# Moving the decoding of the last weights between experts, and three weight splits into the conv layer

## The chip, the core and the metric

The kernel runs on one core of one Trainium2 chip. The metric is the device time of one execution in microseconds (us): 430.35 as the median of 3 runs of the kernel before (429.88 to 430.53). Engines: PE is TensorE, ACT is ScalarE, DVE is VectorE, POOL is GpSimd, SP is SyncE, which here issues DMAs.

## What is computed

Three layers stand one behind the other, on 2 sequences of 768 tokens with 512 values each: a linear attention with decay, a mixture of 8 experts of which each token takes one, and a gated conv layer. Cut to what matters here:

```python
def _moe_ref(x, w_gate, w_local, w1, w2):
    ...
            e = ...                          # one expert for each token
            h = np.maximum(x[b, s] @ w1[e], 0.0)
            out[b, s] = p[e] * (h @ w2[e])

def _moe2_ref(x, w_in, conv_w, w_out):
    h = np.maximum(x @ w_in, 0.0)            # 512 -> 1024
    ...                                      # conv_out: 3 taps along the tokens
    gate = 1.0 / (1.0 + np.exp(-conv_out))
    return (h * gate @ w_out)                # 1024 -> 512
```

w1 is 8 x 512 x 1024, w2 is 8 x 1024 x 512, w_in is 512 x 1024 and w_out is 1024 x 512.

## The kernel before

**Products in three parts.** Every product of the two later layers is made from two parts of each operand: a high part `hi` (ACT copies the f32 value into the reduced f32r type) and the rest `lo` (DVE subtracts `hi` from the value). PE adds hi x hi, hi x lo and lo x hi. For weights this is a split: `split_first` (line 174) makes `whi` on ACT, `split_second` (line 183) makes `wlo` on DVE and then asks for the next load, and `split_unit` does both. A unit is a tile of 128 x 1024 values. There are 64 units of expert weights, 8 for each expert (4 of w1, 4 of w2), loaded by SP into a ring of 4 raw tiles, and then 8 units of the conv layer (4 of w_in, 4 of w_out). `whi` and `wlo` lie in rings of 10 tiles each, so a split waits until PE is done with the unit ten places before it.

**Decoding.** w_in and w_out arrive as 64-bit floats and have to be decoded into f32 first. `decode` (lines 198 to 228) works on half a unit, 128 x 512, 16 times in all. Its first part, `dec_first`, is two ACT instructions (lines 216, 217). Its second part, `dec_second`, is five DVE instructions (lines 219 to 225), two POOL instructions, a product and a sum (lines 227, 228), and a load of 512 KB on SP (line 245) into one of two `draw` tiles. Called with the pool `mo`, the two scratch tiles are one tile `dmf` with two buffers, which it shares with `hr`; called without, they are `dmag` and `df` with one buffer each. The scratch tile `ds` has one buffer. The results are the tiles `wdec`, in the pool `dp`, which is closed before the conv layer.

**The experts.** Experts 1 to 6 run in the first layer `L1(e)` and the second layer `L2(e)`, on 256 tokens. `L1` has four steps `dt` of 24 matmuls; after each but the last a unit is split, and in the last step ACT and DVE make `hh` and `hl`, the two parts of the hidden values, from the banks. Then `T(e + 1)` turns the next expert's tokens (`xsh`, `xsl`), one or two units are split, and `L2` has four steps `j` of 12 matmuls with a split after each. Experts 0 and 7 run in `alone`, in two halves of 128 tokens: four steps for each half `f` of the hidden values (line 652), then ACT's `hr` (line 663), turned back by PE (line 640) into `hh` and `hl`, then eight steps `ft` (line 671), and at the end the result `ys`, half copied by DVE, half by ACT, and stored. `alone` yields after each step, and the calling loop puts other work between. In expert 0 a branch for overflowing tokens (`overflow`) is passed over in this data; its body names the same buffers as `ys`, `hr` and `dmf`.

**Where the decodings stand before.** Expert 0: two, at steps 5 and 6 of its first half. `L1(e)`: one begun at step 2 for e > 1, ended in `L2(e)` at step 1. `L2(e)`: one begun at step 3, ended at step 0 of the next `L1`. Expert 7: three, begun at steps 1, 5 and 10 of its first half. That is 2 + 5 + 6 + 3 = 16.

**Into the conv layer.** After the first half of expert 7, POOL gathers the first sequence's rows (`c_gather`, line 954); during the second half `c_scale` scales them (tiles 0 to 3 on DVE, 4 and 5 on ACT), and `c_T` turns them (line 936) into a bank of the ring "a", which has two banks; ring "b" has three. ACT and DVE read the bank out into the window tiles `x` (lines 946, 949). The last six splits, of which four are of w_out, stand in this half too. The conv layer, `moe2`, runs `h2` (line 979: 12 matmuls for one hidden tile, then `hs`, `cs`, `sg`, `gh` and `gl` on ACT and DVE) and `o2` (line 1031), in the order h2(0, all), h2(1, first four), o2(0), h2(1, last four), o2(1) and so on.

Each engine runs its instructions in the order in which the program writes them, and so do the DMA queues; the order is written out by hand.

Of the kernel before, what the change touches and what calls it, by code (L numbers as in the profile page):

```python
# [8 lines left out]
F32 = mybir.dt.float32  # L9
# [13 lines left out]
E = 8  # L23
P = 128
# [18 lines left out]

WBUFS = 10
DEC_STEP = 10
SPLIT_STEPS = (4, 5, 6, 7, 8, 9)
# [53 lines left out]
def tile_kernel(ctx: ExitStack, tc: tile.TileContext, consts, qk, kv, w1, w2, w_in, conv_w, w_out, out):  # L100
# [87 lines left out]
    def split_unit(engine=None):  # L188
        if nxt["split"] < len(units):
            split_first()  # L190
            split_second(engine or nc.vector)
# [3 lines left out]
    dp = dst.enter_context(tc.tile_pool(name="dp", bufs=1))  # L195
    wdec = [dp.tile([P, 1024], F32, name=f"wdec{j}") for j in range(KD + KF // 2)]

# [64 lines left out]
    def dec_second(queue=nc.sync):  # L262
        if "g" in dec_raw:
            for _ in dec_raw.pop("g"):
                pass
            dec_load(queue)
# [336 lines left out]
    def moe(mo):  # L603
# [25 lines left out]
        def alone(e, half, free):  # L629
# [37 lines left out]
            for ft in range(KF):  # L667
                wh, wl = split[e * 8 + KD + ft // 2]
                ws = slice((ft % 2) * DM, (ft % 2 + 1) * DM)
                for a, b_ in ((hh, wh), (hh, wl), (hl, wh)):  # L670
                    nc.tensor.matmul(yp, lhsT=a[:, ft, sl], rhs=b_[:, ws], start=(ft == 0 and a is hh and b_ is wh),  # L671
                                     stop=(ft == KF - 1 and a is hl))
                if ft == 0:
                    back(1)
                if ft % 2 and free:
                    split.pop(e * 8 + KD + ft // 2)
                    split_unit()
                if ft < KF - 1:
                    yield
# [10 lines left out]
        def L1(e):  # L690
# [3 lines left out]
            for dt in range(KD):  # L694
                wh, wl = split[e * 8 + dt]
                if dt == 0:
                    dec_second()
                elif dt == 1:
                    next(rest, None)
                elif dt == 2 and e > 1:  # L700
                    dec_first(mo)
# [18 lines left out]
        def L2(e):  # L720
# [3 lines left out]
            for j in range(KF // 2):  # L724
                wh, wl = split[e * 8 + KD + j]
                if j == 1:
                    dec_second()
                elif j == 2:
                    next(rest, None)
                elif j == 3:  # L730
                    dec_first(mo)
                for jj in range(2):
# [41 lines left out]
        for n, _ in enumerate(first):  # L774
            if n in (0, 1, 2, 5):
                split_unit(nc.vector)
            if n == 4:
                T(0, (1,))
            if n == 3:
                overflow(mo)  # L780
            if n == 5:
                dec_first()
            elif n == 6:
                dec_first(mo)
            elif n == 7:
                dec_second()
# [15 lines left out]
        e = E - 1  # L802
        for n, _ in enumerate(alone(e, 0, False)):
            if n in (1, 5, 10):
                dec_first()
            if n in (3, 8, 13):
                dec_second()
        raw0 = [dp.tile([P, 2, DM], F32, name="yg0", tag="draw", bufs=2) for _ in range(2)]
# [4 lines left out]
        for n, _ in enumerate(alone(e, 1, True)):  # L813
            if n >= 8 and n - 8 < NC:
                c_scale(n - 8)
            if n == 7:
                window(1, [wp.tile([P, 1024], F32R, name="x2", tag=tag) for tag in ("whi", "whi", "wlo", "wlo")])
            if 10 <= n < 14:
                c_T(0, n - 10)

# [110 lines left out]

    def c_T(b, c):
        y = yg_t.pop(b * NC + c)
        p_ = bank("a")
        for dt in range(KD):
# [22 lines left out]
    def moe2(fo):  # L958
# [98 lines left out]
        for ft in range(KF):  # L1057
# [3 lines left out]
            if 1 <= ft <= NC:  # L1061
                c_gather(NC - 1 + ft, fo.tile([P, DM], F32, name="yg", tag="yg", bufs=6))
        h2(1, 0, KF // 2)
        drain()
# [154 lines left out]
```

## Time and profile before

| what | value |
|---|---|
| median of 3 runs | 430.35 us (429.88 to 430.53) |
| the profiled execution, device time | 430.57 us |
| its span, first to last instruction | 428.8 us |
| PE busy | 394.6 us, 92% of the span |
| DVE busy | 285.7 us, 67% |
| ACT busy | 250.9 us, 59% |
| POOL busy | 114.3 us, 27% |
| PE's share of the chain that ended last | 64% |

Busy shares are means over the whole span. The stages have different limits, so the table by stretches, the chain and the timeline of single engines have to be read beside them. In a timeline the bracket behind an instruction is the time for which its engine sat idle before it, and what ended that. The granted clock of PE is 1.00 at 2.4 GHz and 0.50 at 1.2 GHz.

### The profile page before, as it was taken

The page shows a single profiled execution, that of the slowest core. Times are in us where ns is not written, and L with a number is a line of the kernel's source. Part 1 is how long each engine was busy: PE and PEld are TensorE (multiplying, and loading weights), DVE is VectorE, ACT ScalarE, POOL GpSimd, SP SyncE. Part 2 cuts the span into 40 slices and gives each one's busy share as a digit, 9 for nine tenths or more (in the row PEclk, how much of TensorE's full clock was granted, in tenths as well). Part 3 has the DMA queues.
Part 4 walks back from the last instruction along what each step waited for, and adds up shares of the span by engine and source line. Part 5 has one row for each costly group of instructions (what it writes and reads, how often), then busy time and mean ns, then how long its engine had stood idle before and what let it go on. Part 6 is the DMA issues. An engine that isn't in the chain of part 4 may idle for free.

```text
span 428.8 us, 7360 instructions
## 1 busy us (share of the span) xinstructions
PE 394.6 (92%) x2772; PEld 340.3 (79%) x2772; DVE 285.7 (67%) x540; ACT 250.9 (59%) x489; POOL 114.3 (27%) x109
## 2 busy tenths in 40 slices
PE   5989898949999999999999949779999999999996
PEld 2778776637989898988989828559988989998986
DVE  1457877766797999887778764676990734992250
ACT  3777654627475766566756531657875635982441
POOL 3343450334005044554644442715000000000000
PEclk9999999997999999999999987999999999999999
DMA  7999995376869797888886140324101001001001
GB/s 265 305 318 354 383 326 209 110 240 240 300 213 300 216 311 277 303 281 273 289 266 224 53 141 0 99 74 125 48 0 75 1 26 50 2 0 49 26 0 73
DMA packets 28231, 73.37 MB, mean 171 GB/s; under 512 B 3025, under 2 KB 3793, under 8 KB 28194
## 3 DMA queue, kind: packets, MB, share of 16 engines
q1 hardware_dynamic: 19506, 54.67, 37.2%
q10 hardware_dynamic: 6384, 10.68, 6.8%
q0 software_dynamic: 2304, 7.54, 5.9%
q8 instruction: 22, 0.36, 0.3%
q14 instruction: 15, 0.12, 0.1%
HBM read 62.39 MB, written 10.49 MB: 170 GB/s over the span
## 4 chain that ended last, share of the span: by engine, by line
PE 64%; DVE 5%; ACT 3%; issue 2%; DMA 2%; POOL 2%; ACTq 0%; POOLq 0%; DVEq 0%
PE c L739 15%; PE c L1031 14%; PE b L979 9%; PE b L707 8%; PE rt L979 4%; PE state L707 4%; PE rt L707 4%; PE a L583 1%; PE b L1031 1%; PE c L671 1%; DMA raw<-in_moe_w_dram 1%; DMA yg<-scr,posi 1%; PE a L936 1%; DVE ds L222 1%; DVE wlo L183 1%
## 5 line engine op out<-in xcount | busy, mean ns | idle before, releaser
L183 DVE TENSOR_TENSOR wlo<-raw,whi 128x1024 fp32r<-128x1024 f32 x64 | 81.2, 1282 | 23.4 <-ACT whi L174 22.0
L174 ACT CAST whi<-raw 128x1024 fp32r<-128x1024 f32 x64 | 66.8, 1054 | 39.3 <-PE c L739 22.1
L998 DVE SCALAR_TENSOR_TENSOR cs<-hs,cw,cs 128x384 f32<-128x384 f32 x64 | 39.6, 620 | 32.9 <-ACT cs L996 31.8
L227 POOL TENSOR_TENSOR dmf<-dmf,ds 128x512 f32<-128x512 f32 x12 | 23.2, 1934 | 90.6 <-DVE ds L225 60.1
L739 PE MATMUL c<-whi,hh 128*112 128x512 f32 x96 | 38.0, 396 | 0.0
L979 PE MATMUL b<-x,whi 128*128 128x386 f32 x168 | 35.8, 341 | 1.9 <-ACT x L946 1.6
L739 PE MATMUL c<-wlo,hh 128*112 128x512 f32 x96 | 37.5, 390 | 0.0
L1031 PE MATMUL c<-whi,gh 128*128 128x512 f32 x88 | 35.0, 398 | 0.0
L1031 PE MATMUL c<-whi,gl 128*128 128x512 f32 x88 | 34.8, 395 | 0.0
L1031 PE MATMUL c<-wlo,gh 128*128 128x512 f32 x88 | 34.7, 394 | 0.0
L979 PEld LDWEIGHTS b<-x,whi 128*128 128x128 f32 x168 | 29.5, 189 | 3.3 <-ACT x L946 2.1
L739 PE MATMUL c<-whi,hl 128*112 128x512 f32 x96 | 29.6, 390 | 0.0
L707 PE MATMUL b<-xsh,whi 128*128 128x240 f32 x96 | 26.5, 276 | 0.0
L707 PE MATMUL b<-xsl,whi 128*128 128x240 f32 x96 | 26.5, 276 | 0.0
L707 PE MATMUL b<-xsh,wlo 128*128 128x240 f32 x96 | 26.3, 274 | 0.0
L611 POOL DMA_INDIRECT xg<-scr,permi x15 | 18.4, 1227 | 25.8 <-DVE nbi L542 18.8
L357 DVE TENSOR_TENSOR A<-b,C 128x512 f32<-128x512 f32 x24 | 15.5, 686 | 14.3 <-PE b L351 14.3
L228 POOL TENSOR_TENSOR wdec<-dmf 128x512 f32<-128x512 f32 x12 | 22.5, 1871 | 0.9
L1002 ACT ACTIVATE sg<-cs 128x384 f32<-128x384 f32 x32 | 16.7, 522 | 8.4 <-DVE gl L1008 8.0
L739 PEld LDWEIGHTS c<-whi,hl 128*112 128x112 f32 x96 | 17.4, 181 | 4.5
L739 PEld LDWEIGHTS c<-whi,hh 128*112 128x112 f32 x96 | 17.4, 181 | 4.3
L739 PEld LDWEIGHTS c<-wlo,hh 128*112 128x112 f32 x96 | 17.4, 181 | 4.2
(228 smaller groups left out, 1025.9 us busy)
## 6 DMA issues: line engine op xcount, KB each, us to landing
raw<-in_moe_w_dram SPq DMA_DIRECT2D x64, 512.0 KB, 5.4
qk<-in_qk_dram SPq DMA_DIRECT2D x11, 512.0 KB
kv<-in_kv_dram SPq DMA_DIRECT2D x11, 512.0 KB, 6.8
draw<-in_moe_w_in_dram SPq DMA_DIRECT2D x8, 512.0 KB, 5.7
draw<-in_moe_w_out_dram SPq DMA_DIRECT2D x8, 512.0 KB, 5.4
scr<-xo ACTq DMA_DIRECT2D x11, 256.0 KB, 5.7
out_dram<-os ACTq DMA_DIRECT2D x11, 256.0 KB, 2.6
scr<-ys ACTq DMA_DIRECT2D x10, 256.0 KB
```

The lines of the kernel that those rows point to most:

```text
L174: nc.scalar.copy(hi, raw[u])
L183: engine.tensor_tensor(out=lo, in0=t, in1=hi.bitcast(F32), op=ALU.subtract)
L227: nc.gpsimd.tensor_tensor(out=f, in0=f, in1=s.bitcast(F32), op=ALU.mult)
L228: nc.gpsimd.tensor_tensor(out=out, in0=f, in1=a.bitcast(F32), op=ALU.add)
L357: nc.vector.tensor_tensor(out=A_t[i][j], in0=sc2[j].rearrange("p (a t) -> p a t", a=NP), in1=cv("mask").unsqueeze(1).to_broadcast([P, NP, ...
L611: nc.gpsimd.indirect_dma_start(out=t, out_offset=None, in_=xrow, in_offset=bass.IndirectOffsetOnAxis(ap=permi[:, col:col + 1], axis=0))
L707: nc.tensor.matmul(o, lhsT=a[:, fs], rhs=b_[:, dt, OFF:], start=(dt == 0 and n == 0 and ft % 2 == 0), stop=(dt == KD - 1 and n == 2), skip ...
L739: nc.tensor.matmul(yp[t][0:P - o], lhsT=a[:, ft, t * P + o:(t + 1) * P], rhs=b_[:, ws], start=(ft == 0 and a is hh and b_ is wh), stop=(ft ...
L979: nc.tensor.matmul(pb[:, 0:WN], lhsT=split[u_in + dt][wi][:, fs], rhs=x_[dt // 2][:, dt % 2, :], start=(n == 0), stop=(n == 3 * KD - 1))
L998: nc.vector.scalar_tensor_tensor(out=cs, in0=tap[j], scalar=cw[:, j, ft:ft + 1], in1=cs, op0=ALU.mult, op1=ALU.add)
L1002: nc.scalar.activation(out=sg, in_=cs, func=AF.Sigmoid)
L1031: nc.tensor.matmul(ops[t][:, 0:n_], lhsT=a[:, ts_], rhs=b_[:, ws], start=(ft == 0 and n == 0), stop=(ft == KF - 1 and n == 2))
```

## The change

The 16 decodings are dealt out anew: one in expert 0; two in each of experts 1 and 2 (begun in `L1` at step 2 and in `L2` at step 3); three in each of experts 3, 4 and 5 (`L1` at steps 0 and 2, `L2` at step 2); two in expert 6 (`L1` at steps 0 and 2); none in expert 7. From expert 3 on each is ended one step after it begins, apart from that of `L1`'s step 2, which is ended at step 1 of `L2`. The last three units (`KEPT`) are no longer split in expert 7 but in the conv layer: one after h2(0) has done tile 5, two within the first part of h2(1). Their `wdec` tiles lie in the pool `cst`, which stays open. `c_T` in expert 7 uses the rings "a" and "b" in turn, and the scalings on ACT (tiles 4 and 5) come after the turning of tiles 2 and 3, not before.

```diff
+DENSE = 3
+KEPT = 3
...
-    wdec = [dp.tile([P, 1024], F32, name=f"wdec{j}") for j in range(KD + KF // 2)]
+    n_dec = KD + KF // 2
+    wdec = [(dp if j < n_dec - KEPT else cst).tile([P, 1024], F32, name=f"wdec{j}") for j in range(n_dec)]
...
                 if ft % 2 and free:
                     split.pop(e * 8 + KD + ft // 2)
-                    split_unit()
+                    if nxt["split"] < len(units) - KEPT:
+                        split_unit()
...
                 if dt == 0:
                     dec_second()
+                    if e >= DENSE:
+                        dec_first(mo)
                 elif dt == 1:
                     next(rest, None)
-                elif dt == 2 and e > 1:
+                    dec_second()
+                elif dt == 2:
                     dec_first(mo)
...
                 elif j == 2:
                     next(rest, None)
+                    if DENSE <= e < E - 2:
+                        dec_first(mo)
                 elif j == 3:
-                    dec_first(mo)
+                    if e < DENSE:
+                        dec_first(mo)
+                    else:
+                        dec_second()
...
             if n == 5:
                 dec_first()
-            elif n == 6:
-                dec_first(mo)
             elif n == 7:
                 dec_second()
...
-        for n, _ in enumerate(alone(e, 0, False)):
-            if n in (1, 5, 10):
-                dec_first()
-            if n in (3, 8, 13):
-                dec_second()
+        for _ in alone(e, 0, False):
+            pass
...
         for n, _ in enumerate(alone(e, 1, True)):
-            if n >= 8 and n - 8 < NC:
+            if 8 <= n < 12:
                 c_scale(n - 8)
...
             if 10 <= n < 14:
-                c_T(0, n - 10)
+                c_T(0, n - 10, "ab"[n % 2])
+            if n in (12, 13):
+                c_scale(n - 8)
...
-    def c_T(b, c):
+    def c_T(b, c, ring="a"):
         y = yg_t.pop(b * NC + c)
-        p_ = bank("a")
+        p_ = bank(ring)
...
+            if ft == 5:
+                split_unit()
-        h2(1, 0, KF // 2)
+        for ft in range(KF // 2):
+            h2(1, ft, ft + 1)
+            if ft in (0, 2):
+                split_unit()
         drain()
```

## Rows read from the trace of the kernel before

**Rows 1.** Stretches: length, busy PE, PEld, DVE, ACT, POOL (instructions), PE clock, DMA share, GB/s.

```profile
90.70:97.20 6.50, 0.00 (x0) 0.00 (x0) 4.07 (x6) 2.20 (x5) 4.29 (x4) 0.79 0.51 177
97.20:101.10 3.90, 3.85 (x11) 3.23 (x12) 2.94 (x3) 2.54 (x4) 2.77 (x3) 0.50 0.46 161
...
176.00:198.60 22.60, 22.60 (x154) 20.35 (x154) 18.30 (x25) 14.71 (x20) 11.73 (x7) 1.00 0.86 286
243.80:285.90 42.10, 29.91 (x129) 21.90 (x127) 24.84 (x44) 18.73 (x35) 18.84 (x15) 0.92 0.27 81
257.50:261.50 4.00, 3.96 (x12) 3.29 (x13) 2.12 (x5) 0.59 (x1) 0.00 (x0) 0.50 0.00 0
285.90:313.00 27.10, 26.88 (x152) 25.85 (x153) 21.72 (x51) 20.81 (x45) 6.00 (x6) 1.00 0.23 68
313.00:428.80 115.80, 112.22 (x577) 99.88 (x576) 56.52 (x113) 61.20 (x129) 0.00 (x0) 1.00 0.07 28
```

**Rows 2.** The chain that ended last: start, length in us, what.

```profile
105.27 2.76 PE c L671 x12
...
165.04 10.95 PE c L739 x48
...
187.69 10.95 PE c L739 x48
```

**Rows 3.** Timelines around the first expert's wait: start, length, engine, instruction [idle before].

```profile
90.76 0.67 ACT L216 ACTIVATE dmf<-draw 128x512 f32<-128x512 f32 x1 [4.35 <-DMA raw<-in_moe_w_dram]
...
90.81 1.28 POOL L227 TENSOR_TENSOR df<-df,ds 128x512 f32<-128x512 f32 x1 [6.54 <-remote]
...
95.21 0.42 DVE L681 COPY ys<-c 128x256 f32<-128x256 f32 x1
...
97.25 1.11 PE L640 MATMUL a<-C,hr 128*128 128x128 f32 x4 [6.59 <-ACT hr L663]
```

**Rows 4.** Timelines of the last expert: PE, ACT and POOL.

```profile
253.66 0.49 PE L671 MATMUL c<-whi,hl 128*128 128x512 f32 x1 [2.47 <-DVE hl L644]
257.54 1.11 PE L640 MATMUL a<-C,hr 128*128 128x128 f32 x4 [3.38 <-ACT hr L663]
...
255.79 0.66 ACT L216 ACTIVATE dmag<-draw 128x512 f32<-128x512 f32 x1 [5.82 <-POOL wdec L228]
...
271.90 1.19 POOL L954 DMA_INDIRECT yg<-scr,posi  x1 [0.79 <-DMA scr<-ys]
```

**Rows 5.** Timelines of POOL and DVE where their instructions meet.

```profile
180.88 2.14 POOL L227 TENSOR_TENSOR dmf<-dmf,ds 128x512 f32<-128x512 f32 x1 [3.55 <-DVE ds L225]
...
182.53 1.58 DVE L183 TENSOR_TENSOR wlo<-raw,whi 128x1024 fp32r<-128x1024 f32 x1 [0.66 <-ACT whi L174]
...
252.92 0.68 DVE L644 TENSOR_TENSOR hl<-a,hh 128x512 fp32r<-128x512 f32 x1
...
253.15 1.27 POOL L227 TENSOR_TENSOR df<-df,ds 128x512 f32<-128x512 f32 x1 [1.62 <-DVE ds L225]
```

**Rows 6.** Timeline of DVE in expert 3: a decoding, splits, `hl`.

```profile
156.40 0.41 DVE L219 TENSOR_SCALAR dmf<-dmf 128x512 f32<-128x512 f32 x1
...
158.71 1.22 DVE L183 TENSOR_TENSOR wlo<-raw,whi 128x1024 fp32r<-128x1024 f32 x1
...
164.68 1.21 DVE L714 SCALAR_TENSOR_TENSOR hl<-b,hh 128x480 fp32r<-128x480 f32 x2
...
168.14 2.35 DVE L183 TENSOR_TENSOR wlo<-raw,whi 128x1024 fp32r<-128x1024 f32 x2
```

**Rows 7.** Timelines of DVE and PE at the start of the conv layer.

```profile
292.45 0.26 DVE L964 MEMSET hs<- 128x1 f32 x8 [2.63 <-DMA scr<-ys]
...
300.82 1.26 DVE L998 SCALAR_TENSOR_TENSOR cs<-hs,cw,cs 128x384 f32<-128x384 f32 x2
...
302.94 1.27 DVE L998 SCALAR_TENSOR_TENSOR cs<-hs,cw,cs 128x384 f32<-128x384 f32 x2
...
304.43 0.98 PE L979 MATMUL b<-x,whi 128*128 128x386 f32 x4 [0.17 <-ACT hs L993]
```

## The prediction

> **What bounds the kernel now.** I read three views, in this order. The table by stretches [rows 1] shows where TensorE (PE) is idle or slow: it is full in the middle experts, loses 6.5 us in the first expert, runs 3.9 us after that at half clock, and is busy for only 29.91 of 42.1 us in the last expert. From 313 on it is full for 112.22 of 115.8 us, and the change does not reach that far. The chain of waits [rows 2] says the same of the middle: from one second layer to the next (165.04 to 187.69) it holds nothing but PE, and an expert there takes 22.65 us. The timeline then tells who is late. In the first expert PE waits 6.59 us for `hr` [rows 3]: ScalarE (ACT) sits 4.35 us in front of the second decoding's `dmf` and runs it at 90.76; VectorE (DVE) does the five decode steps next and copies `ys` only at 95.21; ACT's half of `ys` and then `hr` follow, and PE goes on at 97.25. GpSimd (POOL) comes free at 90.81. In the last expert [rows 4] ACT waits 5.82 us for POOL, because `dmag` and `df` have one buffer each, and `hr`, queued behind, keeps PE waiting 3.38 us and leaves it at half clock from 257.5 to 261.5 [rows 1].
>
> **The sum's base.** The profiled execution took 430.57 us, 428.8 of it the span; the median of the runs is 0.22 lower. I sum against 430.57 and take 0.2 off at the end.
>
> **First expert: one decoding fewer.** With `dmf` gone, ACT's next work is `ys`, and DVE's copy of `ys` follows the first decoding. Both `ys` and `hr` use buffers that the skipped overflow branch also names, as `dmf` does; `dmf` started at 90.76, together with POOL [rows 3], so I take it that `ys` too can be written from 90.7 only. From the DVE copy to PE's restart it took 97.25 - 95.21 = 2.04 us; from 90.75 that gives 92.8. PE is 4.45 us earlier, and waits some 2.1 us, less than the 2.47 us of [rows 4]; the one matmul after that wait took 0.49 us and shows no half clock. So the 3.9 us at clock 0.50 [rows 1] go too; they hold about 1.95 us of full-clock work, 1.9 saved. I take 0.5 off for `hl`, which then comes late as slow matmuls no longer cover it. Sum 5.8. If `ys` does not wait for POOL, 2 us more (7.8); if the clock falls all the same, 3.9.
>
> **Last expert: no decodings.** Work of PE in the 42.1 us: 96 matmuls at 2.76/12 = 0.23 [rows 2] are 22.1 us, and eight groups of four transposes with their restart about 0.5 each, 4.0. The rest, 16 us, is waits and half clock. What waits remain I follow by queues: `hr` of the second half is ready 0.2 to 0.3 late twice; `hl` 0.1; the gathers `yg` wait for the landed store of `ys` (POOL's first, 271.90 [rows 4]); with ACT free that store goes out some 3 us earlier in its half, and I place the first gather about 4 us into the second half. By the spacing of POOL's issues and some 3.7 us to land, the first gathered tile is scaled about 0.5 us after PE could turn it, the next ones 0.5, 0 and 0.3. Together 1.9. The stage takes 28.0 instead of 42.1: 14.1 gained. A lower bound counts only the idle time shown and the clock: 12.19 + 2.0 - 1.9 = 12.3. The two bank rings cost nothing: they remove the wait of a third turned tile for the first one's readers, and the five banks are read out before the conv layer comes round to them. The later place of ACT's scalings takes a DMA wait from in front of the copies that the conv layer starts on. I take 14.0.
>
> **Three splits into the conv layer.** Each is a copy on ACT and 1.17 us on DVE (2.35 for two [rows 6]), now queued behind DVE work that repeats every 2.12 us (300.82 to 302.94 [rows 7]), as long as PE's 12 matmuls. The cover is the lead: `hs` starts 6.5 us after PE's first conv matmul (292.45 against 285.9 [rows 1, 7]), since it waits for the last `ys` store; without two splits ahead of that store I get 3.7. DVE starts 2.8 earlier, pays 1.2 before PE needs the bank it waited for at 304.43 [rows 7], so the loss around that wait (about 0.9 of restart and idle) goes. The second and third split are ready 1.8 us before the output layer's matmuls that read them. Gain 0.9; with the cover gone the three would cost up to 3.5. The three tiles in the constant pool move no time.
>
> **Experts 1 to 6: the decodings that come in.** This decides. One decoding is 2.31 us on DVE (156.40 to 158.71 [rows 6]), 1.3 on ACT, two POOL products and one 512 KB load, whose issue on SP waits for the DVE step and has later weight loads behind it. ACT is busy 14.71 and DMA 0.86 of an expert [rows 1]; with four weight tiles loaded ahead and eight units split ahead I cost those two at nothing. DVE is not free. The POOL product takes 1.27 us alone (253.15) and 2.14 beside a split (180.88 to 183.02); the split that began at 182.53 ended at 184.11, 1.09 us after the product's end: it had waited until then [rows 5]. So a split or a decode step and a POOL product do not run at the same time. The PSUM-reading `hl` at 252.92 took its normal 0.68 beside a POOL product [rows 5]; those two do overlap.
>
> The Trainium skill (SBUF — State Buffer, "Who interferes with whom") states it as a rule against this move: DVE and GpSimd share one port pair, held for a whole instruction, and a DVE instruction with two SBUF inputs or in a two-port mode blocks and is blocked, one with a single SBUF input is not. The rows agree in both halves. By the rule and by the rows the sum below is the same; without it, it would be the first rival's.
>
> DVE's work for one of experts 3 to 5: eight splits at 1.17 = 9.4; `hl` and `xsl` 3.5 (164.68 to 168.14 [rows 6]); three decodings 6.9; together 19.8 where PE needs 22.65. To that come POOL's six products. In program order they fall behind the splits of steps 1 (first layer), 1 and 3 (second layer); five stand before DVE work that needs the port, one beside `hl`. Five times 1.27, less 0.07 by which DVE's instructions overlap, are 6.0. So DVE needs 25.8 us, 3.1 more than PE. With two decodings it is 17.5 plus at most 4.8: 22.3, which fits, and the row shows 18.30 busy [rows 1]. The excess reaches PE because `hl` of the next second layer stands in DVE's queue behind it: PE needs it 0.91 us (four matmuls) after that layer starts.
> - Expert 2 gets expert 1's added decoding as a backlog; most of it fits in DVE's gaps: 0.6 (0 to 0.9).
> - Expert 3: before, `hl` starts at 164.68 and is ready at 165.3 [rows 6]; PE needs it at 165.04 + 0.91 = 165.95 [rows 2], 0.65 spare. Now a decoding and a blocked product (2.31 + 1.2) stand ahead of it: 2.9 late; with a backlog from expert 2 up to 4.3. I take 3.6.
> - Experts 4, 5 and 6 each pay the period's excess, 3.1, for the decode steps between one `hl` and the next: 9.3. Were every POOL product hidden beside PSUM work as far as that reaches, the port alone would need 9.4 + 6.9 + 7.6 = 23.9, and the excess is 1.2 each: 3.6.
> - Waits of 3 us may let the clock fall. In the middle that is no addition, since DVE sets the period; after the last wait it can cost 1.9 (as after 97.2 [rows 1]). The row nearest is the 2.47 without a fall; I take 0 and keep 1.9 in the range.
> Loss 13.5, between 6.6 and 17.4.
>
> **Sum.** 5.8 + 14.0 + 0.9 - 13.5 = 7.2 gained: 430.57 - 7.2 - 0.2 = 423.2. With all terms at their ends it is 414 (7.8 + 14.1 + 0.9 - 6.6 gained) to 435 (3.9 + 12.3 - 3.5 - 17.4); they will not all lie at one end, so the forecast's own range is 415.5 to 428.5.
>
> **Rivals.**
> - *DVE hides the added decodings.* If POOL slips into DVE's gaps as it does today, an expert needs 18.30 + 2.31 + 0.4 (half of the 0.8 that 18.30 holds above the bare 17.5) = 21.0, under 22.65; only expert 3 pays, some 1.5. Gain 20.7 - 1.5 = 19.2: 411.2. For it: all middle experts show PE without a wait today. Against: the port's own 23.9.
> - *POOL holds DVE longer*, the slower side. If each product keeps the port for the 2.14 us that its row lists, the period is 19.8 + 5 x 2.14 = 30.5, the excess 7.8: three times that and 4.8 for experts 2 and 3 are 28.2 against 20.7 gained, 437.8. It turns slower where the excess passes (20.7 - 4.2)/3 = 5.5 us an expert. Against: the split at 182.53 ended one split's length after the product, so its extra 0.87 was POOL's own wait.
> - *The first expert's wait does not come from the decoding.* If `hr` is held by the skipped branch in another way, 5.8 shrinks to about 1: 428.
> - *The change doesn't do what it says there*: if the last expert's wait simply becomes one for the gathers, each taking twice the 1.19 us of the row at 271.90 [rows 4], the fourth tile comes 3.6 us later: 423.2 + 3.6 = 427.
>
> **How the numbers follow.** Forecast 0.62, DVE hides it 0.18, POOL holds longer 0.06, first expert unchanged 0.07, gathers 0.05, something else near no change 0.02. Forecast and the two smaller cases on its slow side are 0.74; the range has to reach the hidden case: 410.5 to 428.5 us. About 0.2% (0.9 us) is what a measurement of this kernel can tell from no change. Slower: 0.06, and 0.01 of the forecast's end: 0.07. Within: 0.04. Faster: 0.89.
>
> **What would show it.** Right: in the waits, PE's second-layer matmuls behind DVE's `hl` in experts 3 to 6, about 3 us each, none before; DVE busy for all but a few tenths of some 25.8 us there; PE's wait in the first expert about 2 us with the clock at full rate; no ACT wait for `wdec`; the last expert in some 28 us; `hs` under 4 us after PE's first conv matmul. Wrong: middle experts still at 22.65 us (then 411), or over 28 (then no gain); a wait of `ys` or `hr` past 91 in the first expert; output-layer matmuls that wait for the three moved splits.

## The result, and the profile after

The changed kernel takes 424.69 us (median; 424.09 to 427.31) where the kernel before took 430.12 on the same chip: a ratio of 0.9881, 95% interval 0.9841 to 0.9921. It is faster, by 5.4 us where 7.2 were forecast (423.2 us), and inside the range. The ratios are estimated from all runs of a series; they are not the quotients of the medians given beside them.

The profiled execution took 427.31 us, the longest of its runs, and 425.5 of it are the span; the stretches below are of that one. Line numbers are 2 to 12 higher than before: L643 and L666 turn back and make `hr`, L714 and L751 are the two layers, L720 and L721 `hh` and `hl`, L988 and L1040 the conv layer's two products, L1054 its copy `os`.

| stretch, from a PE matmul to the next named one | before, us | after, us | change | forecast |
|---|---|---|---|---|
| to the start of expert 0's second half | 86.30 | 85.41 | -0.9 | 0 |
| to the first matmul of expert 1 | 21.57 | 17.03 | -4.5 | -5.8 |
| experts 1 to 6 | 135.92 | 150.42 | +14.5 | +13.5 |
| last expert | 42.13 | 28.23 | -13.9 | -14.0 |
| conv layer to the end of its first output half | 43.88 | 45.41 | +1.5 | -0.9 |
| the rest | 99.00 | 99.00 | 0 | 0 |

The sum is -3.3, from 428.8 to 425.5. The first line holds nothing that was changed and shows how far two executions differ. The stretches differ too where the code is the same: in six kernels of the experiments that keep this first expert, the second line is 14.0 to 17.0 us (4.6 to 7.6 gained), and in four that keep these experts 1 to 6, the third is 148.8 to 150.8 (12.9 to 14.9 lost). PE is busy for 397.5 us (93%), DVE 295.4 (69%), ACT 249.4, POOL 118.3. In the chain that ended last PE's share fell from 64% to 55%, and DVE holds 22% of it, with the splits alone (L185) at 8.3%.

The table by stretches, with the columns of [rows 1]: the first expert behind its wait, experts 1 to 6 one by one, the last expert, the conv layer up to its first output half and that half, and two stretches within experts 3 and 6.

```profile
92.00:95.20 3.20, 3.16 (x10) 2.68 (x11) 2.24 (x3) 2.46 (x3) 2.69 (x3) 0.50 0.27 77
...
102.40:125.10 22.70, 22.70 (x154) 20.41 (x154) 19.25 (x27) 14.76 (x21) 3.08 (x2) 1.00 0.77 247
125.10:147.70 22.60, 22.59 (x152) 20.09 (x151) 20.21 (x29) 14.42 (x21) 8.61 (x6) 1.00 0.83 281
147.70:177.50 29.80, 26.21 (x156) 22.54 (x155) 27.90 (x36) 15.51 (x22) 15.44 (x10) 0.89 0.77 259
177.50:201.30 23.80, 22.82 (x154) 20.23 (x153) 21.83 (x30) 15.61 (x22) 12.12 (x8) 1.00 0.85 275
201.30:226.30 25.00, 22.93 (x154) 20.34 (x153) 24.25 (x30) 15.60 (x22) 14.82 (x9) 1.00 0.84 275
226.30:252.90 26.60, 24.54 (x154) 21.43 (x153) 24.46 (x30) 14.46 (x20) 13.79 (x7) 0.94 0.43 138
252.90:281.10 28.20, 26.81 (x130) 20.54 (x128) 12.57 (x22) 13.10 (x26) 7.15 (x6) 1.00 0.28 84
281.10:307.50 26.40, 26.40 (x152) 26.06 (x153) 21.20 (x50) 21.47 (x44) 6.02 (x6) 1.00 0.24 70
307.50:326.50 19.00, 17.04 (x73) 13.46 (x73) 10.74 (x19) 13.24 (x25) 0.00 (x0) 1.00 0.08 28
...
164.60:171.00 6.40, 6.36 (x16) 4.87 (x17) 5.50 (x8) 1.79 (x2) 2.50 (x3) 0.55 0.73 224
241.10:247.00 5.90, 5.88 (x19) 4.51 (x20) 5.68 (x9) 1.05 (x1) 0.54 (x1) 0.71 0.02 6
```

The last expert answers to the row of 42.10 us in [rows 1]: PE is busy for 26.81 of 28.20 us, at full clock, where it was for 29.91 of 42.10. Experts 1 and 2 are still full. From expert 3 on PE is busy for less than its stretch, and DVE for 92 to 97% of it: 24.25 of 25.00 us in expert 5. The clock stands at 0.50 behind the first expert's wait, and is below 1.00 in parts of experts 3 and 6 (a mean of 0.55 and 0.71 in the two stretches).

PE's timeline of the same kernel shows the waits behind that (start, length, engine, instruction [idle before]): one in the first expert, one for ACT and one for DVE in expert 3, one for DVE in each of experts 4 to 6, one in the conv layer. Nothing answers to the last expert's 2.47 and 3.38 us of [rows 4].

```profile
92.04 1.11 PE L643 MATMUL a<-C,hr 128*128 128x128 f32 x4 [2.27 <-ACT hr L666]
...
162.09 0.48 PE L751 MATMUL c<-whi,hh 128*112 128x512 f32 x1 [2.23 <-ACT hh L720]
...
164.64 1.20 PE L751 MATMUL c<-whi,hl 128*112 128x512 f32 x2 [1.36 <-DVE hl L721]
165.63 0.63 PE L751 MATMUL c<-whi,hh 128*112 128x512 f32 x1
...
191.18 0.71 PE L751 MATMUL c<-whi,hl 128*112 128x512 f32 x2 [0.98 <-DVE hl L721]
191.73 0.40 PE L751 MATMUL c<-whi,hh 128*112 128x512 f32 x1
...
216.15 0.72 PE L751 MATMUL c<-whi,hl 128*112 128x512 f32 x2 [2.06 <-DVE hl L721]
...
241.12 0.72 PE L751 MATMUL c<-whi,hl 128*112 128x512 f32 x2 [2.06 <-DVE hl L721]
...
320.83 0.50 PE L1040 MATMUL c<-whi,gh 128*128 128x512 f32 x1 [1.96 <-ACT os L1054]
321.17 0.39 PE L1040 MATMUL c<-wlo,gh 128*128 128x512 f32 x1
```

The same matmul takes 0.63 us at 165.63 and 0.40 at 191.73: the first runs at half clock, the second, behind a wait of 0.98, does not.

Who is late in experts 4 to 6 stands in the timelines of DVE and POOL between two `hl`:

```profile
190.48 1.21 DVE L721 SCALAR_TENSOR_TENSOR hl<-b,hh 128x480 fp32r<-128x480 f32 x2
...
196.21 0.41 DVE L222 TENSOR_SCALAR dmf<-dmf 128x512 f32<-128x512 f32 x1
...
198.52 3.45 DVE L185 TENSOR_TENSOR wlo<-raw,whi 128x1024 fp32r<-128x1024 f32 x2
201.90 1.51 DVE L222 TENSOR_SCALAR dmf<-dmf 128x512 f32<-128x512 f32 x1
...
215.45 1.21 DVE L721 SCALAR_TENSOR_TENSOR hl<-b,hh 128x480 fp32r<-128x480 f32 x2
...
198.75 2.14 POOL L230 TENSOR_TENSOR dmf<-dmf,ds 128x512 f32<-128x512 f32 x1 [4.67 <-DVE ds L228]
200.97 2.16 POOL L231 TENSOR_TENSOR wdec<-dmf 128x512 f32<-128x512 f32 x1
...
214.52 2.14 POOL L231 TENSOR_TENSOR wdec<-dmf 128x512 f32<-128x512 f32 x1
```

From one `hl` to the next it is 24.97 us, and PE needs 22.65. Beside a POOL product two splits take 3.45 us instead of the 2.35 of [rows 6], and the first decode step 1.51 instead of 0.41: each time 1.10 more. `hl`, which reads a bank, keeps its 1.21 although POOL's product of 214.52 runs beside it.

### The profile page after: what moved, and what is told of

The parts are those of the page before. It is cut to its first block, busy times and chain, and to the rows that moved or that the text cites. A ratio compares the mean times of both kernels' runs of the same rounds, so it can differ in the third digit from the quotient of the medians.

```text
span 425.5 us, 7365 instructions
## 1 busy us (share of the span) xinstructions
PE 397.5 (93%) x2772; PEld 341.9 (80%) x2772; DVE 295.4 (69%) x540; ACT 249.4 (59%) x489; POOL 118.3 (28%) x109
## 4 chain that ended last, share of the span: by engine, by line
PE 55%; DVE 22%; ACT 8%; issue 4%; DMA 4%; POOL 3%; ACTq 1%; another core or an unknown queue 0%; DVEq 0%; POOLq 0%; SPq 0%
PE c L751 13%; PE c L1040 12%; DVE wlo L185 8%; PE b L988 8%; PE rt L988 3%; DVE cs L1007 3%; PE c L674 3%; DMA qk<-in_qk_dram 2%; PE b L655 2%; ACT whi L176 2%; PE a L382 2%; PE b L354 2%; DVE sg L1012 1%; PE b L714 1%; POOL qk L333 1%
## 5 line engine op out<-in xcount | busy, mean ns | idle before, releaser
L185 DVE TENSOR_TENSOR wlo<-raw,whi 128x1024 fp32r<-128x1024 f32 x64 | 88.2, 1396 | 11.3 <-ACT whi L176 10.8
L230 POOL TENSOR_TENSOR dmf<-dmf,ds 128x512 f32<-128x512 f32 x15 | 31.3, 2084 | 80.6 <-DVE ds L228 40.9
L751 PE MATMUL c<-whi,hh 128*112 128x512 f32 x96 | 39.7, 413 | 2.2 <-ACT hh L720 2.2
L751 PE MATMUL c<-wlo,hh 128*112 128x512 f32 x96 | 39.2, 408 | 0.0
L988 PE MATMUL b<-x,whi 128*128 128x386 f32 x176 | 37.1, 340 | 0.8 <-ACT x L955 0.8
L751 PE MATMUL c<-whi,hl 128*112 128x512 f32 x96 | 31.7, 413 | 6.5 <-DVE hl L721 6.5
L1040 PE MATMUL c<-whi,gh 128*128 128x512 f32 x88 | 35.1, 399 | 2.0 <-ACT os L1054 2.0
L1040 PE MATMUL c<-whi,gl 128*128 128x512 f32 x88 | 34.8, 395 | 0.0
L1040 PE MATMUL c<-wlo,gh 128*128 128x512 f32 x88 | 34.7, 394 | 0.0
L988 PEld LDWEIGHTS b<-x,whi 128*128 128x128 f32 x176 | 31.1, 189 | 1.4 <-ACT x L955 1.2
L751 PEld LDWEIGHTS c<-whi,hl 128*112 128x112 f32 x96 | 18.1, 193 | 13.1 <-DVE hl L721 8.7
L231 POOL TENSOR_TENSOR wdec<-dmf 128x512 f32<-128x512 f32 x15 | 27.1, 1806 | 1.2
L714 PE MATMUL b<-xsh,whi 128*128 128x240 f32 x96 | 26.5, 276 | 0.0
L714 PE MATMUL b<-xsl,whi 128*128 128x240 f32 x96 | 26.5, 276 | 0.0
L714 PE MATMUL b<-xsh,wlo 128*128 128x240 f32 x96 | 26.3, 274 | 0.0
L614 POOL DMA_INDIRECT xg<-scr,permi x15 | 17.4, 1160 | 24.6 <-DVE nbi L545 17.7
L751 PEld LDWEIGHTS c<-whi,hh 128*112 128x112 f32 x96 | 18.3, 190 | 7.2 <-ACT hh L720 2.5
L751 PEld LDWEIGHTS c<-wlo,hh 128*112 128x112 f32 x96 | 18.4, 191 | 4.7
```

Source lines behind the costliest of these rows:

```text
L185: engine.tensor_tensor(out=lo, in0=t, in1=hi.bitcast(F32), op=ALU.subtract)
L230: nc.gpsimd.tensor_tensor(out=f, in0=f, in1=s.bitcast(F32), op=ALU.mult)
L231: nc.gpsimd.tensor_tensor(out=out, in0=f, in1=a.bitcast(F32), op=ALU.add)
L614: nc.gpsimd.indirect_dma_start(out=t, out_offset=None, in_=xrow, in_offset=bass.IndirectOffsetOnAxis(ap=permi[:, col:col + 1], axis=0))
L714: nc.tensor.matmul(o, lhsT=a[:, fs], rhs=b_[:, dt, OFF:], start=(dt == 0 and n == 0 and ft % 2 == 0), stop=(dt == KD - 1 and n == 2), skip ...
L751: nc.tensor.matmul(yp[t][0:P - o], lhsT=a[:, ft, t * P + o:(t + 1) * P], rhs=b_[:, ws], start=(ft == 0 and a is hh and b_ is wh), stop=(ft ...
```

## The experiments

All edits are to the changed kernel. Ratios are to the kernel before, taken on the same chip in the same series; the changed kernel itself stands at 0.9881 (0.9841 to 0.9921), so that a single experiment has to lie well away from that to be told from it by the whole time. In the experiments' rows line numbers are up to 3 higher.

### Is it the port that DVE and POOL share?

Theory: the period is DVE's work and the time for which POOL's products hold the port. Rival: the lateness comes from elsewhere (ACT, the draw loads), and the products cost nothing. One kernel leaves POOL's products out in decodings 6 to 16, the other has DVE do them.

```diff
+        short = pool is not None and dnx["run"] > 5
+        nc.scalar.activation(out=out if short else f, in_=lo.bitcast(U32), func=AF.Copy, scale=2.0 ** -52)
...
+        if short:
+            return
         nc.gpsimd.tensor_tensor(out=f, in0=f, in1=s.bitcast(F32), op=ALU.mult)
```

> The eleven decodings from expert 3 on leave out their two GpSimd instructions; ScalarE writes its scaled low word straight into wdec, so those weights are not decoded. VectorE's five steps, the loads and all places stay. If GpSimd's hold on the shared port makes the waits: VectorE needs 19.8 us an expert, under PE's 22.65, the waits for hl in experts 4 to 6 (0.98, 2.06, 2.06 us) and the half clock behind them go, and only what ScalarE's wait for the draw load costs in expert 3 stays: 414 to 417 us. If VectorE's own five steps make them: no change, 424 to 425. If the loads of the decodings make them: expert 3 keeps its 3.6 us, 418 to 420.

Measured 415.9 us, ratio 0.9679 (0.9647 to 0.9711): 2.0% under the changed kernel, some 8.7 us. In its trace PE has no wait of 0.3 us or more in experts 4 to 6, experts 4 and 5 take 22.65 us each, and `hl` follows `hl` in 22.61 us; expert 3 keeps a wait of 2.17 us for ACT's `hh`. DVE's rows of that kernel:

```profile
187.12 1.21 DVE L724 SCALAR_TENSOR_TENSOR hl<-b,hh 128x480 fp32r<-128x480 f32 x2
...
209.73 1.21 DVE L724 SCALAR_TENSOR_TENSOR hl<-b,hh 128x480 fp32r<-128x480 f32 x2
```

```diff
+        last = nc.vector if pool is not None and dnx["run"] > 5 else nc.gpsimd
-        nc.gpsimd.tensor_tensor(out=f, in0=f, in1=s.bitcast(F32), op=ALU.mult)
-        nc.gpsimd.tensor_tensor(out=out, in0=f, in1=a.bitcast(F32), op=ALU.add)
+        last.tensor_tensor(out=f, in0=f, in1=s.bitcast(F32), op=ALU.mult)
+        last.tensor_tensor(out=out, in0=f, in1=a.bitcast(F32), op=ALU.add)
```

> The same eleven decodings, with product and sum on VectorE instead of GpSimd; the result is the full one. If GpSimd's hold on the port costs VectorE about 1.2 us for each of five instructions an expert: those 6.0 us become six instructions of about 0.65, 3.9, so an expert of three decodings takes about 23.7 us instead of 25.0, expert 6 likewise: 4 to 5 us faster than the changed kernel, 419.5 to 421. If GpSimd costs VectorE little and VectorE's own work is what is late: 3.9 us more in each of experts 3 to 6, 434 to 438.

Measured 421.2 us, ratio 0.9851 (0.98 to 0.9901). DVE's timeline in expert 4 shows the two added steps and the splits behind them, and PE's the waits that are left:

```profile
195.32 0.69 DVE L231 TENSOR_TENSOR dmf<-dmf,ds 128x512 f32<-128x512 f32 x1
196.04 0.69 DVE L232 TENSOR_TENSOR wdec<-dmf 128x512 f32<-128x512 f32 x1
196.65 2.35 DVE L185 TENSOR_TENSOR wlo<-raw,whi 128x1024 fp32r<-128x1024 f32 x2
...
211.72 0.71 PE L752 MATMUL c<-whi,hl 128*112 128x512 f32 x2 [0.96 <-DVE hl L722]
235.58 0.72 PE L752 MATMUL c<-whi,hl 128*112 128x512 f32 x2 [0.95 <-DVE hl L722]
```

DVE does seven tenths of a microsecond of work in place of POOL's 1.09 of hold, nothing is stretched any more, the period is 23.86 us, and the waits of 2.06 have become 0.96. DVE with more work of its own is on time earlier: that decides for the port. The whole time does not tell this kernel from the changed one, since its interval takes in 0.9881; in the trace experts 1 to 6 take 145.0 us where they took 148.8 to 150.8 with the products on POOL, about the 4 to 5 us that were expected.

### The first expert: the decoding, and the branch

One kernel puts the second decoding back into expert 0; the other lets POOL issue the gathers of expert 1 behind the skipped branch instead of ahead of it.

```diff
             if n == 5:
                 dec_first()
+            elif n == 6:
+                dec_first(mo)
             elif n == 7:
```

> The changed kernel with the second decoding put back into expert 0, where the kernel before had it; the other decodings move up by one, so that expert 6 has one fewer. If the gain of the first expert comes from the decoding that left it, the wait of TensorE for hr there is 6 to 7 us again, with half clock behind it, and the time from the end of that wait to the first matmul of expert 1 is about 10.6 us as before; the middle experts keep their waits but for the last one, for hl in expert 6 (2.06 us), which shrinks by about a decoding. Sum: 4.5 us lost, 2 to 4 gained back with the last wait and the half clock that followed it: a ratio to the kernel before of 0.986 to 0.994. Rival, that the wait is set by the skipped branch alone, whatever is decoded: about 2.3 us again and a ratio under 0.986.

Measured 430.39 us, ratio 1.0001 (0.9967 to 1.0034), outside the 0.986 to 0.994 that were expected.

```profile
94.91 1.11 PE L643 MATMUL a<-C,hr 128*128 128x128 f32 x4 [5.25 <-ACT hr L666]
...
323.93 0.70 PE L1042 MATMUL c<-whi,gh 128*128 128x512 f32 x1 [1.98 <-ACT os L1056]
324.42 0.63 PE L1042 MATMUL c<-wlo,gh 128*128 128x512 f32 x1
```

PE waits 5.25 us for `hr`, and 10.62 us pass from there to expert 1's first matmul, as before. The expectation for the last wait failed: `hl` in expert 6 still comes 2.08 us late, since the decoding that fell away is begun behind it. The two ratios differ by 0.012, some 5 us, but not all of that is the price of the first expert's decoding: between the two traces it is 3.2 us (20.24 for 17.03 in the second line of the table). Another 1.6 lie in the conv layer, where the wait for `os` is as long as in the changed kernel but half clock follows it here (0.63 us for a matmul that took 0.39 there).

```diff
         gather(0, (1,))
-        gather(1)
...
             if n == 3:
                 overflow(mo)
+                gather(1)
```

> Expert 1's two gathers on GpSimd stand behind the branch for overflowing tokens instead of in front of it; the rest is the changed kernel. If GpSimd leaves the branch only when its gathers have landed, and ys and hr of the first expert wait for that: one gather is out instead of three, GpSimd's first product starts some 4 us earlier (about 86 instead of 90), PE's wait in front of L643 goes from 2.27 to under 0.5 us and no half clock follows: 1 to 4 us faster than the changed kernel. If ys and hr wait for the decoding on VectorE or for instruction fetch: no change in that wait.

Measured 423.32 us, ratio 0.9841 (0.9787 to 0.9895); the interval takes in the changed kernel's ratio, so the verdict is the trace's. POOL and DVE in the first expert, first of the changed kernel, then of this one:

```profile
90.00 0.42 DVE L685 COPY ys<-c 128x256 f32<-128x256 f32 x1 [2.05 <-remote]
90.15 1.26 POOL L230 TENSOR_TENSOR df<-df,ds 128x512 f32<-128x512 f32 x1 [7.03 <-remote]
```

```profile
87.26 0.42 DVE L685 COPY ys<-c 128x256 f32<-128x256 f32 x1
87.51 1.29 POOL L230 TENSOR_TENSOR df<-df,ds 128x512 f32<-128x512 f32 x1 [1.59 <-DVE ds L228]
```

With the gathers out of the way, POOL waits for nothing but DVE, `ys` follows the decode step at once, and PE's wait for `hr` is gone. From the restart to expert 1's first matmul it is 9.29 us here, 10.40 in the changed kernel. So what was left of the wait comes from the branch, behind which POOL goes on late with those gathers ahead of it. How late differs between executions: with the gathers ahead and the same first expert, six other kernels here show waits of 0.31, 0.79, 0.81, 1.22, 1.65 and 2.25 us for `hr`; the five with the gathers behind it show 0.16 at most.

### Expert 3: the draw load, or DVE's backlog?

In expert 3 of the changed kernel `hh` comes late because ACT sat 4.73 us in front of a `draw` load. This kernel has the products on DVE as above and begins the decoding of step 2 of expert 3's first layer in its second layer, so that ACT's queue has no `draw` ahead of `hh`.

```diff
-                elif dt == 2:
+                elif dt == 2 and e != DENSE:
                     dec_first(mo)
...
+                if j == 0 and e == DENSE:
+                    dec_first(mo)
                 if j == 1:
                     dec_second()
```

> The kernel with product and sum on VectorE (e7), and in expert 3 the decoding of step 2 of the first layer is begun in the second layer instead. In e7 the wait for hh in expert 3 is 3.44 us, behind ScalarE's wait for a draw load that is issued only two steps earlier. If that load is what is late: that wait goes, hl stays up to 1.5 us late, 2 to 3.5 us faster than e7. If VectorE is late there by as much: the same wait stands at hl, no change.

Measured 423.6 us, ratio 0.9856 (0.9798 to 0.9913): no gain over 0.9851.

```profile
162.18 1.19 PE L754 MATMUL c<-whi,hl 128*112 128x512 f32 x2 [4.20 <-DVE hl L722]
```

The wait for `hh`, 3.44 us with the products on DVE, is gone, and one of 4.20 for `hl` stands in its place. DVE is as late as the load there: the load's issue on SP waits for a DVE step that reads the tile (SP issues it at 153.50 in the changed kernel, when that step of 153.05 is done).

### The conv layer: the splits, the scalings, the rings

```diff
-KEPT = 3
+KEPT = 0
```

> Only the three moved splits are put back into the last expert (KEPT = 0); decodings, rings and scalings stay as changed. By the prediction's term (moving them gains 0.9 us): 425.6. By the trace of the changed kernel, where the output layer's third tile waits 1.96 us for ScalarE's os, which comes after scalings and splits: that wait goes, the last expert gets some 1 us longer, 423.5 to 424.5. If the splits in the last expert hold up the last ys store as before: 1.6 us at the start of the conv layer return, 426 to 427.

Measured 424.27 us, ratio 0.9906 (0.9882 to 0.9929). The wait for `os` (1.96 us) is gone; in its place PE waits 1.74 us for `x` at the start of the layer, 0.83 for `hs` and 0.65 for a scaled tile. Three splits ahead of the layer or in it: a difference of 0.0025, within the intervals. In the traces moving them gains some 1.5 us (174.2 to 172.6 from the last expert's first matmul to the end): the last expert is 1.85 us shorter and the conv layer's way to its output half 1.9, and the output half, with the wait for `os`, 2.2 longer.

```diff
-        if t < 4:
+        if t < 4 or t >= NC:
```

> The scalings of the second sequence's tiles (six, during the first output layer) are on VectorE instead of ScalarE; nothing else. VectorE is idle there from 319 on. If os is late because three scalings of 0.62 us stand in front of it on ScalarE: the wait of 1.96 us shrinks to 0.1 to 0.3, 422.8 to 423.1. If os is late because the drain of the conv layer ends late: the scalings do not matter, 424.2 to 425.

Measured 422.62 us, ratio 0.984 (0.9816 to 0.9865). The second sequence's scalings are on DVE now, and PE's wait for `os` is gone. ACT's timeline around `os`, first of the changed kernel, then of this one:

```profile
317.94 0.52 ACT L1016 CAST gh<-sg 128x384 fp32r<-128x384 f32 x1 [0.23 <-DVE sg L1012]
318.36 1.94 ACT L939 ACTIVATE yg<-yg,G_all 128x512 f32<-128x512 f32 x3
320.21 0.56 ACT L1054 COPY os<-c 128x512 f32<-128x512 f32 x1
```

```profile
317.94 0.58 ACT L1054 COPY os<-c 128x512 f32<-128x512 f32 x1
```

PE waits for the bank that `os` reads out; `os` stands behind three scalings of 1.94 us, and those behind `gh`, which DVE feeds late since it has done three splits. Taking either away takes the wait away. The interval overlaps the changed kernel's; in the trace the output half takes 17.2 us instead of 19.0.

```diff
-            if 8 <= n < 12:
+            if n >= 8 and n - 8 < NC:
                 c_scale(n - 8)
...
-                c_T(0, n - 10, "ab"[n % 2])
-            if n in (12, 13):
-                c_scale(n - 8)
+                c_T(0, n - 10)
```

> The turned tiles go to ring a alone and the scalings on ScalarE stand in front of the turning again, as before; the decodings and the moved splits stay as changed. The prediction costs both at nothing. If they are free: within 0.5 us of the changed kernel, 0.987 to 0.989 of the kernel before. If the third tile's wait for the first one's readers (0.69 and 0.84 us before) and ScalarE's wait for the gathered tile (1.5 us) are worth their size: 1.5 to 3 us slower than the changed kernel.

Measured 425.89 us, ratio 0.9877 (0.9819 to 0.9935), the same as the changed kernel. From the wait for `hl` in expert 6 to the first conv matmul it takes 39.38 us at full clock, where the kernel with the late gathers, at full clock there as well, takes 38.31: ring and order are worth about 1.1 us in the trace, all of it in the last expert (29.26 us for 28.19), which the whole time does not tell from nothing.

### A kernel built from this

Products from expert 3 to expert 6 and the second sequence's scalings on DVE, gathers late, and the decodings dealt more evenly: three only in experts 4 and 5, and one in the last expert's first half.

```diff
-DENSE = 3
+DENSE = 4
...
-        for _ in alone(e, 0, False):
-            pass
+        for n, _ in enumerate(alone(e, 0, False)):
+            if n == 3:
+                dec_first()
+            elif n == 6:
+                dec_second()
```

> Four edits on the changed kernel: product and sum on VectorE from expert 3 on, scalings of the second sequence on VectorE, gathers behind the branch, and expert 3 with two decodings only, the sixteenth being put into the last expert (begun after step 3 of its first half, ended after step 6). Port theory: expert 3 keeps 22.65 us, experts 4 and 5 pay 1 to 2 us each, the last expert stays at 28 us since VectorE is half idle there: 411 to 414 us where the kernel before takes 429. If a decoding in the last expert brings the old waits back: 3 to 6 us more.

Measured 413.6 us, ratio 0.9627 (0.9564 to 0.969). From the first expert on PE waits at most 1.13 us at once, and the clock is 1.00 over the whole run.

> The version that took 0.9627 of the time before, with product and sum of the decodings back on GpSimd: three decodings only in experts 4 and 5, one in expert 7, scalings on VectorE, the gather of expert 1 late. It parts what the even dealing brings from what the move to VectorE brings. By the port theory an expert with three decodings needs about 25.0 us of VectorE and one with two fits into TensorE's 22.65: hl waits of about 2 us in two or three experts, and a time 2 to 5 us above the 413.6 of that version where the clock holds (415.5 to 418.5; ratio 0.967 to 0.975), more where it falls. If products on GpSimd cost nothing (the rival), the time is the same 413.6 within 1 us.

With the products on POOL again: 418.23 us, ratio 0.9736 (0.9695 to 0.9778). The waits for `hl` are 0.96, 1.25 and 2.09 us in experts 4 to 6, and the clock's mean in the stretches behind the waits of experts 4 and 6 is 0.79 and 0.76. So of the 2.5% between the changed kernel and this build, 1.1% is the products' place (0.9736 to 0.9627; the half clock behind the waits is in it), and the rest the dealing, the gathers and the scalings together.

Then two decodings in the last expert, three only in expert 5 (`DENSE = 5`), first with

```diff
+            if n in (1, 5):
+                dec_first()
+            elif n in (3, 8):
+                dec_second()
```

> The same version with products on VectorE and two decodings in expert 7's first half, three in expert 5 alone. If VectorE's queue sets the period only where three decodings stand, the waits of experts 4 (1.13 us for hh) and 5 (0.95 for hl) go, experts 3 to 5 take 22.65 to 23.3 us, and expert 7 keeps its 28 us since VectorE and ScalarE have room there: 1.5 to 2.5 us less than 413.6, about 411.5, ratio 0.958. Rival: the second decoding in expert 7 delays hr there as in the kernel before and costs 2 us or more: 413 to 416.

Measured 416.73 us, ratio 0.9701 (0.9663 to 0.9739): the rival, a little beyond its 413 to 416. Expert 4 falls from 24.47 to 22.65 us, but ACT's and PE's timelines in the last expert show

```profile
248.94 0.66 ACT L219 ACTIVATE dmag<-draw 128x512 f32<-128x512 f32 x1 [2.88 <-POOL wdec L232]
...
250.70 0.66 PE L644 MATMUL a<-C,hr 128*128 128x128 f32 x4 [3.18 <-ACT hr L667]
```

This is the wait of [rows 4] come back: `dmag` and `df` have one buffer, and `hr` stands behind them. With the second decoding at steps 9 and 12, behind the second `hr`:

> The last version with the second decoding of expert 7 begun at step 9 instead of 5 and ended at step 12 instead of 8, behind ScalarE's hr of the second half. In the run before, ScalarE waited 2.88 us for GpSimd's sum there (one buffer of dmag and df) with hr behind it, and TensorE 3.18 us for hr. If that queue place is the cause, both waits go, the last expert takes 28 us again, and the time falls by about 3 us to 413.5 or a little less (ratio 0.960 to 0.964), a little under the version with one decoding in expert 7. Rival: two decodings in expert 7 cost there whatever their place, by the gathers that need the draw tiles: a wait for the turned tiles instead, and 415 to 417.

Measured 412.03 us, ratio 0.9591 (0.956 to 0.9622), the fastest here: 4.1% under the kernel before, 2.9% under the changed one. The wait of 3.18 us is gone, the last expert takes 28.8 us and the clock is 1.00 throughout; the longest waits left from the first expert on are 1.44 us for `hh` and 0.96 for `hl`.

## Why the prediction was right, and where it was not

**Bound and direction: right.** The middle experts pass from PE to DVE's queue, as forecast; PE waits for `hl` from expert 3 on and nowhere before. The rivals are out: the middle experts did not stay at 22.65 us (hidden), a product holds DVE for 1.10 us and not 2.14 (longer), PE's wait in the first expert fell from 6.59 us with its decoding gone, to 2.27, and the last expert took its 28 us (gathers).

**Last expert, 14.0: right.** 28.23 us against 28.0, with waits of 0.4 and 0.2 us for scaled tiles and 0.75 for `x` in front of the conv layer, together 1.3 against 1.9; the forecast waits for `hr` did not come. More than the decodings is in it: with rings and scalings as before the stage takes 29.26 us, with the three splits in it 30.08. The forecast took these waits as gone in its 28.0 and did not price them by themselves.

**The port: right in kind, a little high.** Five blocked products were put at 6.0 us. Between the two `hl` the five instructions that they hold up are stretched by 1.10, 1.10, 0.74, 1.09 and 1.09, together 5.1. The period is 24.97 us, not 25.8, and the excess 2.3, not 3.1. The split (two SBUF inputs) took 3.45 for 2.35 and the decode step (one SBUF input) 1.51 for 0.41; `hl`, which reads a bank and one SBUF tile, kept 1.21. The Trainium skill's rule (SBUF — State Buffer, "Who interferes with whom"), by which two SBUF inputs or a two-port mode contend with GpSimd and one SBUF input otherwise does not, agrees for the split and for `hl`. For the decode step it agrees only if that ran in a two-port mode, which no row shows.

**Experts 1 to 6, 13.5: the sum came out (14.5), two terms did not.** By expert, measured against forecast in the profiled execution: expert 2 0.3 for 0.6; expert 3 6.75 for 3.6; expert 4 1.2 for 3.1; expert 5 2.3 for 3.1; expert 6 3.9 for 3.1. In expert 3 the waits are 2.23 + 1.36 = 3.59 us, the 3.6 of the forecast to the tenth. The rest, 3.2, is the half clock behind them. The step that failed is "In the middle that is no addition, since DVE sets the period": PE lost 3.2 us to the clock and DVE's next `hl` came 26.54 us after the last instead of 24.97, so half of it, 1.6, stayed: with PE slow, DVE sat idle for 3.0 us before splits in between, waiting for ACT's `whi`, and ACT for PE. In expert 6 the fall cost 3.9 - 2.06 = 1.9 us, the bound kept in the range and set to 0 in the sum. Both together are the 3.5 us that make up for a period shorter by 0.8 in three experts (2.4): the sum was right by errors of opposite sign. The stated upper bound, 17.4, is also 1.0 more than its terms give (0.9 + 4.3 + 9.3 + 1.9 = 16.4); nothing hangs on it.

**First expert, 5.8: 4.5 measured.** `ys` waited for POOL until 90.0, and PE's wait was 2.27 against "some 2.1"; the two kernels above show that the decoding and the branch are its causes. That the size fits is in part luck: with the same code the wait was 0.31 to 2.25 us in six other kernels. The step that failed is the clock, taken from the 2.47 us of [rows 4] that had no half clock behind them: after 2.27 us it stood at 0.50 for 3.2 us. Its price is 10.40 - 9.29 = 1.1 us, most of the 1.3 missing. The row had one matmul behind it and then another wait; it was too little to carry the rule.

**Conv layer, +0.9: the stretch lost 1.5; wrong.** The lead shrank (`hs` 4.7 us after the first conv matmul, before 6.5, forecast 3.7), 0.7 us were gained up to the output half (26.41 for 27.08), and no matmul waits for the moved splits. The step that failed is the cover of the splits behind that point: I followed the readers of the splits and not the queue that DVE feeds. ACT's `os` stands behind `gh` and behind three scalings, and came 1.96 us late, which makes the output half 2.2 us longer (19.0 for 16.8). Taken by itself, against the kernel with the splits put back, moving them still gained some 1.5 us in the trace, since it shortens the last expert by 1.85 as well.

**The draw loads, costed at nothing: a second chain of the same length.** In expert 3 ACT waited 4.73 us for one and `hh` came 2.23 late; taking it away gained nothing, since DVE was as late.

What stays open is the difference between the changed kernel's runs (424.09 to 427.31 us). The profiled one, the longest, has three stretches at half clock, which cost about 1.1, 1.6 to 3.2 and 1.9 us. Its mean granted clock was 0.984, that of the others 0.988 to 0.992, so they had less half clock; where, was not seen, since they left no trace. Open is also when a wait is followed by half clock at all.

## What to carry to other kernels

Before moving elementwise work between TensorE-bound stages, sum the queue of VectorE for one stage together with the time for which GpSimd's two-input products keep VectorE out, and put the work down only where that sum stays under TensorE's time: experts 1 to 6 lost 14.5 us to their decodings, and 4.3 (140.2 for 135.9) with three in one expert only and none of the products of experts 3 to 6 on GpSimd. A wait of 2 us of TensorE is to be priced with the half clock that may follow it, half to all of the wait again in this kernel. When work enters a queue, follow not only its readers but what stands behind it in every engine it feeds.

## What the runs showed of the hardware

- The granted clock fell to 0.50 after waits of 2.27 and 2.25 us in the first expert (two kernels), and not after 1.65, 1.22 or 0.81 there. In one run it fell behind a wait of 2.06 us in expert 6 and not behind one of 2.06 in expert 5. The wait for `os`, 1.96 to 1.98 us in seven kernels' profiled runs, had half clock behind it in three of them, which cost 1.6 us, and full clock in four. So the length of the wait alone did not settle it.
- A VectorE `tensor_scalar` with one SBUF input was stretched by a GpSimd product as a two-input subtraction was: 0.41 to 1.51 us and 2.35 to 3.45.
- GpSimd's first product behind the skipped branch started at 90.15 us, after 7.03 us idle, with the two gathers of expert 1 issued ahead of the branch, and at 87.51, after a wait for VectorE alone, with these issued behind it. Over seven kernels with the same first expert and the gathers ahead that idle time was 4.8 to 7.0 us. That the branch waits for gathers to land was not measured by itself.
